# Moving one block's PSUM copies from ScalarE to VectorE, and splitting the last copy and store

## Chip, cores, metric

The kernel runs on one core of a Trainium2 chip. The metric is device time in microseconds (us) of one execution; medians of several executions are given. All executions here are of the undisturbed ("fast") state. The profile is of one execution and its span is about 1.7 us shorter than that execution's device time. Engines: PE is TensorE's matmuls, PEld its weight loads, DVE is VectorE, ACT ScalarE, SPq the queue from which SyncE issues stores.

## The reference

A depthwise causal convolution over seven taps (weights softmaxed per head) is followed by a two-layer feed-forward network with a leaky ReLU:

```python
x_unf = x_pad[:, idx, :].reshape(B, S, K, H, group)      # B=8, S=4096, D=192, H=8, K=7
x = np.einsum('hk,bskhg->bshg', w, x_unf).reshape(B * S, D)
h = x @ w_in                                             # 192 -> 2048
g = np.maximum(0.01 * h, h)
out = (g @ w_out).astype(np.float32)                     # 2048 -> 192
```

## The kernel before

The work is cut into blocks of 512 positions of two batch rows. VectorE convolves (tile `yt`, three chunks of channels, seven steps each), TensorE multiplies by `w_in` into `ph` in PSUM, ScalarE applies the leaky ReLU (`g`), TensorE multiplies by `w_out` into `po`, and a copy brings each finished sum of 128 positions from PSUM to `o_sb`, whence two sums at a time are stored. Blocks 0 to 4 run as two groups of 256, so that TensorE gets its first work early; from block 5 a group is a whole block of 512.

Which engine makes the copy depends on the block:

```python
NHALF = 5
...
def evac_o(n):
    b, e, s = subs[n]                       # block, batch row, 128 positions in the block
    ...
    o_sb = osb[n // 2]
    copy = nc.scalar.copy if b < NHALF else nc.vector.tensor_copy
    copy(out=o_sb[:, n % 2, :], in_=po.pop(n))
    if n % 2 == 1:                          # store two sums together, 192 KB
        nc.sync.dma_start(out=..., in_=osb.pop(n // 2))
```

In the timelines here VectorE and ScalarE run their instructions in the order in which they are written (in the kernel before ScalarE's copy at 121.25 us, below, stands between two pairs of activations). In each step `j` of a group the first matmuls come first, then the second matmuls with the copies that they finish, then the convolution of the next group:

```python
for j in range(steps):
    for u in range(2 * j, 2 * j + 2):
        mm1(grp, u)                         # TensorE -> ph, ScalarE -> g
    for _ in range(quota):
        mm2_slot(slot); slot += 1           # TensorE -> po; evac_o(n) where a sum is done
    ...
    for job in ahead[per * j : per * (j + 1)]:
        job()                               # VectorE: convolution of the next group
```

`ph` has two buffers and `po` four. A copy of one of these sums therefore stands in its engine's queue in front of the convolution steps of the same step `j`.

## Time and profile before

| | before |
|---|---|
| median, 5 executions | 698.27 us (697.35 to 700.79) |
| span of the profile | 696.7 us |
| TensorE busy | 688.9 us, 99% |
| VectorE, ScalarE busy | 542.4 us, 512.3 us |
| TensorE's waits after 100 us | one: 0.83 us on `yt`, ends at 118.99 |
| start of the last copy to the end of the span | 693.07 to 696.7, 3.63 us |

ScalarE's rhythm in block 5, from its timeline (start us, duration us, group, and in brackets the idle time before it and what ended it):

```profile
119.42 1.94 ACT L364 ACTIVATE g<-ph 128x1024 bf16<-128x1024 f32 x2 [1.48 <-PE ph L357]
121.25 0.33 ACT L416 COPY o_sb<-po 128x192 f32<-128x192 f32 x1
121.44 1.97 ACT L364 ACTIVATE g<-ph 128x1024 bf16<-128x1024 f32 x2
123.58 1.94 ACT L364 ACTIVATE g<-ph 128x1024 bf16<-128x1024 f32 x2 [0.16 <-PE ph L357]
```

Four activations and one copy take 123.58 - 119.42 = 4.16 us, two TensorE steps. ScalarE looks full, and yet it waits 0.16 us for TensorE. The last copy, from VectorE's timeline, and the last four stores, from the list of transfers (count, KB each, median us from issue to landing):

```profile
693.07 0.36 DVE L416 COPY o_sb<-po 128x192 f32<-128x192 f32 x1 [0.96 <-PE po L377]
```

```profile
out_dram<-o_sb SPq DMA_DIRECT2D x4, 192.0 KB, 2.0
```

### The profile page before, as it was taken

Reading aid. Unit: us, or ns where it says so; the run is one execution under the profiler, and the core shown is the slowest. Engines: PE = TensorE matmul, PEld = TensorE weight load, DVE = VectorE, ACT = ScalarE, POOL = GpSimd, SP = SyncE. Lnnn points to the kernel's source line nnn. Section 1 sums busy time; section 2 is a strip of 40 time slices with the busy share of each in tenths; the row PEclk is TensorE's granted clock in tenths of the full one; section 3 lists DMA queues with packets and bytes.
Section 4 is the critical chain, followed back from the end, with each engine's and each line's share of the span. In section 5 each row is a group of like instructions: output and inputs, shape, how many; then the busy total and the mean of one; then the engine's idle time right before and its main releaser. Section 6 shows DMA issues by size and latency. Waiting matters only on the chain.

```text
span 696.7 us, 26003 instructions
## 1 busy us (share of the span) xinstructions
PE 688.9 (99%) x11756; PEld 611.7 (88%) x11756; DVE 542.4 (78%) x1000; ACT 512.3 (74%) x576; POOL 142.2 (20%) x199
## 2 busy tenths in 40 slices
PE   8999999999999999999999999999999999999997
PEld 6899998678888888888888888888888888888887
DVE  6899999867777787777787777787777787777712
ACT  6788887977777777777777777777777777777770
POOL 4732221320222220222211222220222210000000
PEclk9999999999999999999999999999999999999999
DMA  9987563754556545556644556544566535122112
GB/s 172 110 106 84 83 88 68 83 77 80 73 67 92 81 70 81 74 67 93 81 67 85 67 74 92 80 73 74 73 75 86 87 66 73 56 52 58 47 36 70
DMA packets 184847, 54.39 MB, mean 78 GB/s; under 512 B 148384, under 2 KB 184736, under 8 KB 184736
## 3 DMA queue, kind: packets, MB, share of 16 engines
q0 software_dynamic: 98768, 14.17, 29.4%
q1 hardware_dynamic: 85968, 38.56, 23.0%
q8 instruction: 92, 1.51, 0.9%
q14 instruction: 19, 0.16, 0.1%
HBM read 29.88 MB, written 25.17 MB: 79 GB/s over the span
## 4 chain that ended last, share of the span: by engine, by line
PE 83%; DVE 12%; DMA 3%; issue 1%; POOL 0%; ACT 0%; POOLq 0%; ACTq 0%
PE po L377 43%; PE ph L357 40%; DVE yt L182 11%; DMA w_out<-in_moe_w_out_dram 2%; DVE yt L176 1%; DMA w_in<-in_moe_w_in_dram 1%; POOL sel L228 0%; ACT g L364 0%; DVE xt L157 0%; POOL sel L226 0%; DVE o_sb L416 0%; POOL ident masks.py:199 0%; PE ptr L143 0%; POOL ident masks.py:197 0%; POOLq masks.py:199 0%
## 5 line engine op out<-in xcount | busy, mean ns | idle before, releaser
L364 ACT ACTIVATE g<-ph 128x1024 bf16<-128x1024 f32 x512 | 496.4, 1021 | 162.9 <-PE ph L357 162.9
L182 DVE SCALAR_TENSOR_TENSOR yt<-xt,wk,yt 128x512 bf16<-128x512 bf16 (+1 forms) x648 | 442.6, 683 | 17.6
L377 PE MATMUL po<-w_out,g 64*128 64x192 bf16 (+1 forms) x8048 | 398.2, 243 | 0.7 <-DMA w_out<-in_moe_w_out_dram 0.7
L377 PEld LDWEIGHTS <-g 64*128 64x128 bf16 (+1 forms) x8048 | 372.5, 94 | 29.4 <-issue 1.1
L357 PE MATMUL ph<-yt,w_in 64*128 64x512 bf16 (+1 forms) x3552 | 392.2, 347 | 2.3 <-ACT g L364 0.9
L357 PEld LDWEIGHTS <-w_in 64*128 64x128 bf16 x3552 | 250.1, 94 | 47.0 <-issue 5.3
L79 POOL DMA_DIRECT2D x_bf<-in_x_dram x180 | 133.6, 777 | 420.0 <-DMA xt<-x_bf 420.0
L416 DVE COPY o_sb<-po 128x192 f32<-128x192 f32 x216 | 77.3, 358 | 127.2 <-PE po L377 124.8
L176 DVE TENSOR_SCALAR yt<-xt,wk 128x512 bf16<-128x512 bf16 (+1 forms) x108 | 36.8, 340 | 0.2
L416 ACT COPY o_sb<-po 128x192 f32<-128x192 f32 x40 | 13.1, 327 | 0.0
L201 PE MATMUL acc<-xt,diag 64*64 64x256 bf16 x84 | 6.6, 319 | 0.0
L201 PEld LDWEIGHTS <-diag 64*64 64x64 bf16 x84 | 5.1, 126 | 1.4 <-issue 0.6
L250 PE MATMUL warm<-zero 128*128 128x256 bf16 x18 | 4.3, 399 | 1.1 <-DVE junk L218 1.1
L238 POOL DMA_DIRECT2D w_in<-in_moe_w_in_dram x8 | 5.1, 644 | 0.0
L157 DVE COPY xt<-ptr 128x384 bf16<-128x384 bf16 x7 | 2.2, 354 | 2.4 <-PE ptr L143 2.4
L250 PEld LDWEIGHTS <-zero 128*128 128x128 bf16 x18 | 2.0, 131 | 2.2 <-DVE junk L218 1.1
L296 ACT ACTIVATE diag<-ident,wkl 128x64 bf16<-128x64 bf16 x14 | 3.6, 336 | 0.0
L128 DVE CAST x_bf<-x_nat 128x384 bf16<-128x384 f32 x5 | 2.4, 499 | 1.4 <-DMA x_nat<-in_x_dram 1.4
L461 POOL COPY pjunk<-g 1x1 bf16<-1x1 bf16 x1 | 0.2, 177 | 12.0 <-ACT g L364 12.0
L128 ACT CAST x_bf<-x_nat 128x384 bf16<-128x384 f32 x3 | 1.5, 506 | 1.5 <-DMA x_nat<-in_x_dram 1.5
L317 ACT ACTIVATE yt<-acc,rsum 128x256 bf16<-128x256 f32 x2 | 0.9, 473 | 2.2 <-PE acc L201 2.2
L255 ACT ACT_TABLE_LOAD x1 | 1.3, 1283 | 0.8 <-PEq L498 0.8
(29 smaller groups left out, 13.7 us busy)
## 6 DMA issues: line engine op xcount, KB each, us to landing
out_dram<-o_sb SPq DMA_DIRECT2D x128, 192.0 KB, 2.1
x_bf<-in_x_dram POOLq DMA_DIRECT2D x180, 64.0 KB, 3.2
x_nat<-in_x_dram SPq DMA_DIRECT2D x8, 192.0 KB, 4.8
w_in<-in_moe_w_in_dram POOLq DMA_DIRECT2D x8, 192.0 KB, 8.7
xt<-x_bf SPq DMA_TRANSPOSE x90, 2.5
w_out<-in_moe_w_out_dram POOLq DMA_DIRECT2D x1, 768.0 KB, 14.7
w<-in_weight_dram SPq DMA_DIRECT2D x1, 0.2 KB
```

What stands on the lines that cost most here:

```text
L79: nc.gpsimd.dma_start(out=t[:, c, :, e, :], in_=src[2 * rp + e, :, :, c * CH : (c + 1) * CH],)
L128: copy(out=x_bf[q // 2][:, :, h * HS : (h + 1) * HS, e, :], in_=x_nat[q][:, e, :, :].rearrange("p s (c k) -> p c s k", c=NCH),)
L176: lambda s=src, d=dst, c=c: nc.vector.tensor_scalar_mul(d, s, wk[:, c, 0:1])
L182: lambda s=src, d=dst, c=c, k=k: nc.vector.scalar_tensor_tensor(out=d, in0=s, scalar=wk[:, c, k : k + 1], in1=d, op0=mybir.AluOpType.mult, ...
L201: lambda k=k, p=p, a=a, e=e, ps=ps: nc.tensor.matmul(out=acc[ps, :T], lhsT=diag[c][ps, p, k, :], rhs=xt[0][ps, c, a : a + T], start=(k == ...
L238: nc.gpsimd.dma_start(out=w_in[e * CH : (e + 1) * CH, :, fs], in_=moe_w_in[:, fs].rearrange("(c p) f -> p c f", p=CH),)
L250: nc.tensor.matmul(out=wa[:, 0, 0:HT], lhsT=zero[:, 0:128], rhs=zero, start=True, stop=True)
L296: act = nc.scalar.activation(out=diag[c][:, 1, k, :], in_=ident2, func=mybir.ActivationFunctionType.Copy, scale=wkl[:, c, k : k + 1],)
L357: nc.tensor.matmul(out=ph[:, e, i * T : (i + 1) * T], lhsT=w_in[ps, c, f * 128 : (f + 1) * 128], rhs=y[ps, c, t0 : t0 + T], start=(c == 0) ...
L364: act = nc.scalar.activation(out=g[blk][:, nf * u : nf * (u + 1), :, t0 : t0 + T], in_=ph.rearrange("p e (i t) -> p i e t", i=nf), func=my ...
L377: ins = nc.tensor.matmul(out=po[m], lhsT=g[b][ps, fc, e, s * 128 : (s + 1) * 128], rhs=w_out[ps, fc, :], start=(rt != 1 and fc == 0), stop ...
L416: copy(out=o_sb[:, n % 2, :], in_=po.pop(n))
```

## The change

Its intent, as far as the edit tells: relieve ScalarE in block 5, where it is nearly full, by giving block 4's eight copies to VectorE, and shorten the end by letting two engines share the last copy and by storing the last two sums one by one.

```diff
-        copy = nc.scalar.copy if b < NHALF else nc.vector.tensor_copy
-        copy(out=o_sb[:, n % 2, :], in_=po.pop(n))
-        if n % 2 == 1:
+        copy = nc.scalar.copy if b < NHALF - 1 else nc.vector.tensor_copy
+        acc = po.pop(n)
+        if n == NSUB - 1:
+
+            nc.vector.tensor_copy(out=o_sb[:, 1, 0 : D // 2], in_=acc[:, 0 : D // 2])
+            nc.scalar.copy(out=o_sb[:, 1, D // 2 : D], in_=acc[:, D // 2 : D])
+        else:
+            copy(out=o_sb[:, n % 2, :], in_=acc)
+        if n >= NSUB - 2:
+            t0 = st * ST + s * 128
+            nc.sync.dma_start(
+                out=out_rows[2 * rp + e, t0 : t0 + 128, :], in_=o_sb[:, n % 2, :]
+            )
+        elif n % 2 == 1:
```

## The prediction

> **What bounds the kernel now.** I read the page first, then the table of stretches, then the waits of TensorE, then the timelines of TensorE and VectorE in the one stretch where the table has a hole, and last the end of the program.
>
> The chain on the page gives TensorE 83% and VectorE 12%:
>
> ```profile
> PE 83%; DVE 12%; DMA 3%; issue 1%; POOL 0%; ACT 0%; POOLq 0%; ACTq 0%
> ```
>
> The table of stretches (length, then busy time of PE, PEld, DVE, ACT, POOL, clock, DMA share, GB/s) says where they change over:
>
> ```profile
> 100.00:110.00 10.00, 10.00 (x219) 10.00 (x216) 9.50 (x18) 8.55 (x12) 3.44 (x5) 1.00 0.76 82
> 110.00:120.00 10.00, 9.17 (x182) 8.35 (x178) 9.56 (x15) 7.08 (x11) 0.49 (x1) 1.00 0.32 80
> 120.00:130.00 10.00, 9.93 (x140) 6.26 (x136) 9.55 (x14) 9.68 (x14) 3.97 (x6) 1.00 0.83 88
> ```
>
> VectorE is at 9.5 of 10 there with no wait; the rest is issue gaps. TensorE has a hole at 110 to 120, and from 120 ScalarE is nearly full. After 140 TensorE is busy without a break until its last matmul. Its list of waits from 100 us on has one entry, 0.8 us on `yt`. TensorE's timeline shows it (start, duration, group, idle before):
>
> ```profile
> 112.27 1.51 PE L357 MATMUL ph<-yt,w_in 64*128 64x256 bf16 x24
> 113.58 1.52 PE L377 MATMUL po<-w_out,g 64*128 64x192 bf16 x32
> 114.90 1.51 PE L357 MATMUL ph<-yt,w_in 64*128 64x256 bf16 x24
> 116.21 1.52 PE L377 MATMUL po<-w_out,g 64*128 64x192 bf16 x32
> 117.53 0.63 PE L357 MATMUL ph<-yt,w_in 64*128 64x512 bf16 x4
> 118.99 1.04 PE L357 MATMUL ph<-yt,w_in 64*128 64x512 bf16 x8 [0.83 <-DVE yt L182]
> ```
>
> At 117.53 block 5 begins, the first block of full 512-wide groups. Its first two pairs use chunks 0 and 1 of the convolution, the third waits for chunk 2. VectorE's timeline shows that chunk's end:
>
> ```profile
> 108.88 0.35 DVE L176 TENSOR_SCALAR yt<-xt,wk 128x512 bf16<-128x512 bf16 x1
> 109.26 4.69 DVE L182 SCALAR_TENSOR_TENSOR yt<-xt,wk,yt 128x512 bf16<-128x512 bf16 x6
> 113.86 0.35 DVE L176 TENSOR_SCALAR yt<-xt,wk 128x512 bf16<-128x512 bf16 x1
> 114.25 4.69 DVE L182 SCALAR_TENSOR_TENSOR yt<-xt,wk,yt 128x512 bf16<-128x512 bf16 x6
> ```
>
> 114.25 + 4.69 = 118.94, and TensorE goes on at 118.99. So until 119 us the end of the program hangs on VectorE, with no slack at all, and afterwards on TensorE. That is exactly where block 4's sums are copied out.
>
> The end: the last sum is copied by VectorE from 693.07 to 693.43, its store (with the sum before it, 192 KB) is issued at 693.46, and the span ends at 696.7. Stores land 2.0 us after issue.
>
> [...] A copy that waits for its sum therefore holds up every convolution step behind it. The trace agrees: at 142.75 VectorE's first copy has 4.64 us of idle time before it, released by TensorE, and the next convolution step starts only at 143.03, 0.28 after the copy's start. [...] ScalarE's half-copy waits for the count that VectorE's half-copy raises. [...]
>
> **Part 1: block 4's eight copies go from ScalarE to VectorE.** By the built order the first (call it sum 32) comes after five of seven steps of chunk 1 of block 5, the next (33) six steps later, three steps before the end of chunk 2. Sum 34 comes directly after block 5's convolution; 35, 36 and 37 after six steps each of block 6, with three steps left; 38 and 39 in block 7. A full step takes 0.787 us start to start, a copy that need not wait 0.28 (142.75 to 143.03).
>
> When is a sum ready? At 142.75 the copy starts 0.93 after its group of sum matmuls began (141.82); its last matmul is the 16th there, as it is for sums 32 to 37. So I add 0.93 to the group's start.
>
> - Sum 32: VectorE gets there when the sixth step of chunk 1 would have started, 109.26 + 4 x 0.787 = 112.41. The sum is ready at 113.58 + 0.93 = 114.51. Wait 2.10, copy 0.28: everything behind it is 2.38 later.
> - Sum 33: reached at 116.61 + 2.38 = 118.99, ready at 116.21 + 0.93 = 117.14. No wait, 0.28. Block 5's chunk 2 ends 2.66 later, at 121.60, and TensorE resumes at 121.65. **First loss: 2.66 us**, all on the path, since slack was nil.
> - Sum 34: its matmul group began at 119.85, now 122.51, ready 123.44. VectorE stands idle from 121.6: 1.84, plus 0.28. Block 6's first step moves from 118.86 to 123.72, by 4.86.
> - Sums 35, 36, 37: reached at 128.0, 132.5, 137.0; ready at 127.7, 131.9, 136.0. No wait, 3 x 0.28 = 0.84.
> - Block 6's convolution ended at 133.9; now 133.9 + 4.86 + 0.84 = 139.6. TensorE began block 6 at 135.19 and needed its chunk 2 two pairs later, 135.62; shifted by 2.66 that is 138.28. It waits again until 139.65. **Second loss: 1.37 us**, so 139.65 - 135.62 = 4.03 in all.
> - Sums 38 and 39 let VectorE wait again (38 by some 1.9 us), but block 7's steps then fall into the rhythm of all later blocks (three steps, 2.36, and a copy, 0.28, per TensorE step of 2.62). By that rhythm block 7's chunk 2 ends at about 159.9, and TensorE needs it at 160.6: no third loss.
>
> What ScalarE gains is hidden. In block 5 a TensorE step takes (135.19 - 120.51) / 7 = 2.10 us, against 0.66 + 1.31 = 1.97 of matmul work; at most 7 x 0.13 = 0.9 us could come back, and ScalarE's copies alternate with waits on `ph`, so they are not the whole cause. But arriving earlier at block 6 only lengthens the second wait, because VectorE sets its end. I count 0.
>
> **Part 2: the last sum in halves.** A half-copy saves 96 columns: about 0.10 us on VectorE (358 to 258 ns), 0.08 on ScalarE (327 to 247). Because they run one after the other with some 0.05 between, copying takes 0.258 + 0.05 + 0.247 = 0.56 instead of 0.36: +0.20. The last store is 96 KB instead of 192. In the last 7 us the stores move at 300 to 325 GB/s, so halving saves about 0.3 of the landing at most[...]. I take -0.25. Together -0.05: a wash.
>
> **Sum:** 697.73 + 4.03 - 0.05 = 701.7 us.
>
> **Rivals.**
> (a) *The intended gain.* ScalarE is 9.68 of 10 busy at 120 to 130, so unloading it could return up to 0.9 us, and the tail 0.3: 696.5. For it: ScalarE's load. Against: VectorE is the engine with nil slack just before, and the copies land in its queue.
> (b) *The copies cost only their own time.* If sums 32 and 34 were ready when VectorE comes, block 5 would start 2 x 0.28 = 0.56 later, block 6 would not wait, and the ScalarE gain could show: 697.4 to 698.3. Against: sum 32's matmuls begin at 113.58, after VectorE is there (112.41). This ordering comes from the trace, so I hold it unlikely.
> (c) [...] TensorE's idle gap grows from 0.83 to about 3.5 us. [...] one chance in ten.
> (d) *The tail alone.* If the halves overlap or the small store lands much faster, -0.5; if the extra handover is slow, +0.3. It moves the sum little either way.
>
> **Range and chances.** The arithmetic of Part 1 is good to a few tenths, run to run scatter likewise (697.35 to 697.73 in two runs, one at 700.79); (c) stretches the upper side. 700.3 to 703.4. A change of 2% is 14 us; nothing here comes near. Faster 0.005, within 2% 0.985, slower 0.01.
>
> **What would show it.** In the changed kernel: VectorE's first copy at about 114.5 with some 2.1 us idle before it, released by TensorE; a TensorE wait on `yt` of about 3.5 us ending near 121.6; a copy at about 123.4 with 1.8 idle before it; a second TensorE wait on `yt` of about 1.4 near 139.6; the last ScalarE copy starting only after VectorE's ends; the last matmuls some 4 us later. Wrong would be: a single wait on `yt` of about 1.4 (then rival b), none or a shorter block 5 (a), or a clock under 1.00 near 122 (c).

## The result

| | before | changed |
|---|---|---|
| median, 5 executions each | 698.27 us | 703.92 us (702.24 to 705.44) |
| span of the profile | 696.7 us | 700.9 us |
| TensorE's waits on `yt` after 100 us | 0.83 | 3.35 and 0.65 |
| mean granted clock in the executions | 0.999 (the profiled one) | 0.998, 0.994, 0.997, 0.995, 0.995 |
| last copy's start to the end | 3.63 | 3.48 |

The ratio is 1.0073, with a 95% interval of 1.0046 to 1.0101: the mean time of one kernel's fast runs over that of the other's of the same rounds, so it is not quite the ratio of the medians. The change makes the kernel about 5 us slower, which is within 2%.

VectorE's timeline in the changed kernel, around block 4's copies (columns as above; lines between are left out):

```profile
108.44 3.11 DVE L182 SCALAR_TENSOR_TENSOR yt<-xt,wk,yt 128x512 bf16<-128x512 bf16 x4
114.17 0.36 DVE L422 COPY o_sb<-po 128x192 f32<-128x192 f32 x1 [2.62 <-PE po L377]
...
118.51 0.35 DVE L422 COPY o_sb<-po 128x192 f32<-128x192 f32 x1
118.78 2.32 DVE L182 SCALAR_TENSOR_TENSOR yt<-xt,wk,yt 128x512 bf16<-128x512 bf16 x3
124.10 0.36 DVE L422 COPY o_sb<-po 128x192 f32<-128x192 f32 x1 [3.00 <-PE po L377]
```

Where six convolution steps followed each other without a break before, VectorE stops after the fifth of chunk 1's seven steps (the four in the first line, after a first one on L176) and waits 2.62 us for sum 32. It waits again, 3.00 us, for sum 34. TensorE's timeline shows what this does to it:

```profile
115.84 1.52 PE L377 MATMUL po<-w_out,g 64*128 64x192 bf16 x32
117.16 0.63 PE L357 MATMUL ph<-yt,w_in 64*128 64x512 bf16 x4
121.15 1.57 PE L357 MATMUL ph<-yt,w_in 64*128 64x512 bf16 x8 [3.35 <-DVE yt L182]
122.48 1.52 PE L377 MATMUL po<-w_out,g 64*128 64x192 bf16 x16
...
138.77 0.61 PE L357 MATMUL ph<-yt,w_in 64*128 64x512 bf16 x4
140.04 1.04 PE L357 MATMUL ph<-yt,w_in 64*128 64x512 bf16 x8 [0.65 <-DVE yt L182]
```

The wait at block 5 has grown from 0.83 to 3.35 us, and there is a second one at block 6. And the matmuls right after the first wait are slow: eight of them last 1.57 us, where the same eight at 140.04 last 1.04. The table of stretches says why (length; busy time of PE, PEld, DVE, ACT, POOL; the last three columns are granted clock, DMA share and GB/s):

```profile
121.00:121.50 0.50, 0.35 (x4) 0.22 (x5) 0.10 (x1) 0.00 (x0) 0.50 (x1) 1.00 0.93 58
121.50:122.00 0.50, 0.50 (x6) 0.19 (x2) 0.00 (x0) 0.42 (x1) 0.50 (x2) 0.52 1.48 94
...
124.50:125.00 0.50, 0.50 (x5) 0.20 (x3) 0.47 (x2) 0.00 (x0) 0.00 (x0) 0.57 0.69 43
125.00:125.50 0.50, 0.50 (x8) 0.30 (x6) 0.50 (x1) 0.29 (x1) 0.00 (x0) 1.00 0.07 4
```

The clock is halved from about 121.5 to 124.9 us. That is why sum 34 comes late and its copy waits 3.00.

ScalarE, relieved of its copies, keeps the same rhythm:

```profile
129.37 3.89 ACT L364 ACTIVATE g<-ph 128x1024 bf16<-128x1024 f32 x4 [0.27 <-PE ph L357]
133.52 3.89 ACT L364 ACTIVATE g<-ph 128x1024 bf16<-128x1024 f32 x4 [0.26 <-PE ph L357]
```

Four activations per 4.15 us, as before with the copy among them; only the wait on `ph` is longer. The end of the program, from the timeline, and its stores from the list of transfers:

```profile
697.42 0.26 DVE L419 COPY o_sb<-po 128x96 f32<-128x96 f32 x1 [0.96 <-PE po L377]
697.72 0.24 ACT L420 COPY o_sb<-po 128x96 f32<-128x96 f32 x1 [12.97 <-DVE o_sb L419]
```

```profile
out_dram<-o_sb SPq DMA_DIRECT2D x2, 96.0 KB, 1.6
```

The halves run one after the other: ScalarE's starts 0.04 us after VectorE's ends.

### The profile page after: what moved, and what is told of

It is laid out like the page before. It is cut to its first block, busy times and chain, and to the rows that moved or that the text cites.

```text
span 700.9 us, 26010 instructions
## 1 busy us (share of the span) xinstructions
PE 689.9 (98%) x11756; PEld 615.2 (88%) x11756; DVE 543.5 (78%) x1008; ACT 511.4 (73%) x569; POOL 142.3 (20%) x199
## 4 chain that ended last, share of the span: by engine, by line
PE 94%; DMA 3%; DVE 2%; ACT 1%; POOL 0%; issue 0%; DVEq 0%; POOLq 0%
PE po L377 48%; PE ph L357 45%; DMA w_out<-in_moe_w_out_dram 2%; DVE yt L182 2%; DMA w_in<-in_moe_w_in_dram 1%; ACT g L364 1%; DVE o_sb L422 0%; POOL sel L228 0%; DVE yt L176 0%; POOL sel L226 0%; POOL ident masks.py:199 0%; DVE o_sb L419 0%; ACT o_sb L420 0%; POOL ident masks.py:197 0%; PE ptr L143 0%
## 5 line engine op out<-in xcount | busy, mean ns | idle before, releaser
L357 PEld LDWEIGHTS <-w_in 64*128 64x128 bf16 x3552 | 253.1, 94 | 48.4 <-issue 8.6
L422 DVE COPY o_sb<-po 128x192 f32<-128x192 f32 x223 | 79.6, 357 | 129.7 <-PE po L377 127.3
L176 DVE TENSOR_SCALAR yt<-xt,wk 128x512 bf16<-128x512 bf16 (+1 forms) x108 | 36.2, 335 | 0.2
L422 ACT COPY o_sb<-po 128x192 f32<-128x192 f32 x32 | 10.5, 327 | 0.0
```

Source lines behind the costliest of these rows:

```text
L176: lambda s=src, d=dst, c=c: nc.vector.tensor_scalar_mul(d, s, wk[:, c, 0:1])
L357: nc.tensor.matmul(out=ph[:, e, i * T : (i + 1) * T], lhsT=w_in[ps, c, f * 128 : (f + 1) * 128], rhs=y[ps, c, t0 : t0 + T], start=(c == 0) ...
L422: copy(out=o_sb[:, n % 2, :], in_=acc)
```

## The experiments

Theory: VectorE reaches the copies of sums 32 and 34 before the sums are ready, its queue stops, and TensorE pays twice on `yt`; the long gap lets the clock fall. Rivals: the copies' own time on VectorE is what costs; the tail costs; the clock falls for another reason.

Times carry a scatter of some 0.5 us and now and then 3 us (the kernel before: 697.25 to 702.10), so I also compare the traces by one number each: the time from the start of block 5's first 512-wide matmul to the start of the last copy. It leaves out the start-up, which varies (that matmul started between 116.9 and 120.1 us), and the tail, which is given apart.

| kernel | median us | before, same rounds | ratio | block 5 to last copy (trace) | tail (trace) | waits on `yt` (trace) | executions with clock under 0.999 |
|---|---|---|---|---|---|---|---|
| before | | | | 575.54 | 3.63 | 0.83 | 5 of 44 |
| changed | 703.92 | 698.27 | 1.0073 | 580.26 | 3.48 | 3.35, 0.65 | 5 of 5 |
| tail only | 698.17 | 698.15 | 0.9992 | 575.35 | 3.48 | 0.64 | 0 of 6 |
| block 4 only | 702.89 | 698.15 | 1.0058 | 579.08 | 3.57 | 3.36, 0.90 | 3 of 6 |
| all but sum 32 | 700.27 | 698.15 | 1.0025 | 577.23 | 3.61 | 1.64, 0.81 | 1 of 6 |
| copies later | 698.64 | 698.15 | 1.0000 | 575.15 | 3.62 | 0.50 | 1 of 6 |
| keep warm | 702.47 | 697.93 | 1.0059 | 578.95 | 3.52 | filled (0.29 left), 0.77 | 0 of 5 |
| changed, again | 703.56 | 697.93 | 1.0078 | 581.09 | 3.52 | 3.35, 0.41 | 5 of 6 |
| store alone | 698.16 | 697.93 | 1.0011 | 575.78 | 3.36 | 1.08 | 2 of 6 |
| alone, early | 698.35 | 697.93 | 1.0003 | 575.41 | 3.35 | 0.38 | 1 of 5 |
| later and alone | 698.38 | 698.69 | 1.0006 | 575.91 | 3.36 | 1.27 | 2 of 6 |
| only sum 32 | 702.13 | 698.69 | 1.0055 | 580.57 | 3.55 | 3.22 | 6 of 6 |
| only sum 34 | 699.44 | 698.69 | 1.0016 | 575.67 | 3.62 | 0.53, 0.35 | 2 of 6 |
| keep warm, again | 701.99 | 697.80 | 1.0058 | 578.94 | 3.49 | filled (0.29 left), 0.77 | 1 of 6 |

All gave correct results. Intervals of the ratios are 0.002 to 0.003 either side. The tails use the span as it is printed, to 0.1 us; with the unrounded spans of the packed traces they are 3.58 to 3.59 us for every old tail, 3.48 to 3.49 for the changed one and 3.31 for the last two sums stored alone with a whole copy. The mean clock falls below 0.999 also through drops in the start-up: the traces of "alone, early" and "only sum 34" have one at 25 to 30 us, after a wait of 2.04 and 2.12 us for `w_out`. The half clock after the last matmul counts in it too (in the kernel before from 695.9 us to the end at 696.7); it alone brings the profiled execution of the kernel before to 0.999.

### Tail only

The change without its first line: `b < NHALF` is kept.

```diff
-        copy = nc.scalar.copy if b < NHALF - 1 else nc.vector.tensor_copy
+        copy = nc.scalar.copy if b < NHALF else nc.vector.tensor_copy
```

> Only the tail of the change: last sum copied in two halves, last two sums stored alone; block 4's copies stay on ScalarE. Theory (the tail is a wash, the loss is all in block 5 and 6): the halves run one after the other and end 0.18 us later than one copy would (0.258 + 0.04 + 0.238 against 0.358), the small store lands in 1.6 instead of 2.0 us; span from the last copy's start to the end 3.48 instead of 3.63, so about 0.15 us faster than before, not to be told from it by time. No new wait on yt, clock as before (0.999). Rival (the tail's new waits cost what was lost): several us slower.

Measured: same time, 3.48 us of tail against 3.63 (0.10 less with the spans unrounded), one wait on `yt` of 0.64. As expected; the tail is not where the time went.

### Block 4 only

```diff
-        copy = nc.scalar.copy if b < NHALF else nc.vector.tensor_copy
+        copy = nc.scalar.copy if b < NHALF - 1 else nc.vector.tensor_copy
```

> Only block 4's eight copies on VectorE, tail as before. Theory: the whole loss, 4 to 6 us slower than before; VectorE's copy of sum 32 with 2.1 to 2.6 us idle before it, a TensorE wait on yt of about 3.4 us, a half-rate clock[...] just after it, sum 34's copy with 2 to 3 us idle before it, a second wait on yt of 0.5 to 1.4. Rival (the tail): same as before.

Measured: 4.7 us slower by the medians. The trace happened to catch an execution with full clock (1.00), in spite of the gap, so it shows the two waits by themselves:

```profile
121.74 1.04 PE L357 MATMUL ph<-yt,w_in 64*128 64x512 bf16 x8 [3.36 <-DVE yt L182]
...
139.45 1.04 PE L357 MATMUL ph<-yt,w_in 64*128 64x512 bf16 x8 [0.90 <-DVE yt L182]
```

Between block 5 and the last copy 579.08 - 575.54 = 3.54 us are lost, and 3.36 + 0.90 - 0.83 = 3.43 of them are these waits. The copies of sums 32 and 34 waited 1.95 and 1.85 us. The expected wait of 2.1 to 2.6 for sum 32 was a little too high. The half-rate clock is not certain: 3 of 6 executions had it.

### All but sum 32

```diff
-        copy = nc.scalar.copy if b < NHALF else nc.vector.tensor_copy
+        copy = nc.scalar.copy if n <= (NHALF - 1) * 2 * SUB else nc.vector.tensor_copy
```

> Sums 33 to 39 on VectorE, sum 32 stays on ScalarE, tail as before. Theory (it is the wait in front of the copy of sum 32, not the copies' own time, that makes the long gap, and the gap that drops the clock): first TensorE wait on yt 0.83 + 0.28 = 1.1 us, no clock drop, sum 34's copy still waits about 1.8 us, second wait on yt about 1.2 us: some 1.5 us slower than before. Rival (the copies' own time, 0.28 each, is what counts): nearly the loss of the full change for seven of eight copies, that is 4 us or more, or the clock drops here as well.

Measured: 2.1 us slower by time, 1.69 by the trace. The first wait was 1.64 and not 1.1, since sum 33 was not ready either, which the expectation had overlooked: VectorE, no longer held up by sum 32, reached that copy at 116.60 and waited 0.89 us for it. The copy of sum 34 waited 1.84, as expected. No clock drop in the trace. Seven of the eight copies cost less than half; the rival of the copies' own time falls.

### Only sum 32

```diff
-        copy = nc.scalar.copy if b < NHALF else nc.vector.tensor_copy
+        copy = nc.scalar.copy if b < NHALF and n != (NHALF - 1) * 2 * SUB else nc.vector.tensor_copy
```

> Only sum 32 is copied by VectorE, the other seven of block 4 by ScalarE; tail as before. Theory (the first loss alone): copy of sum 32 with 2.0 to 2.6 us idle before it; wait on yt at block 5 about 3.1 us, that is 0.28 less than in the changed kernel (sum 33's copy); no second wait on yt; in some executions a half-rate clock after it. In the trace 2.4 us lost if the clock holds, up to 4 if it drops; time 2 to 4 us slower than before. Rival (losses need all the copies): under 1 us.

Measured: 3.4 us slower for one moved copy of 0.36 us. VectorE's and TensorE's timelines:

```profile
113.99 0.36 DVE L416 COPY o_sb<-po 128x192 f32<-128x192 f32 x1 [1.82 <-PE po L377]
```

```profile
116.98 0.63 PE L357 MATMUL ph<-yt,w_in 64*128 64x512 bf16 x4
120.83 1.89 PE L357 MATMUL ph<-yt,w_in 64*128 64x512 bf16 x8 [3.22 <-DVE yt L182]
```

There is no second wait, as expected. All six executions had a low clock. In the trace the clock is halved from 119.9 to 126.7, and 5.0 us are lost between block 5 and the last copy, more than the 4 I allowed: of these, 3.22 - 0.83 = 2.4 are the wait and the other 2.6 lie in the stretch of half clock, which no second wait absorbs here.

### Only sum 34

```diff
-        copy = nc.scalar.copy if b < NHALF else nc.vector.tensor_copy
+        copy = nc.scalar.copy if b < NHALF and n != (NHALF - 1) * 2 * SUB + 2 else nc.vector.tensor_copy
```

> Only sum 34 is copied by VectorE, the other seven by ScalarE; tail as before. Theory (the second loss alone): first wait on yt as before (0.6 to 1.1 us), copy of sum 34 with about 1.84 us idle before it, block 6's convolution 2.1 us later, second wait on yt 0.1 to 0.7 us because block 6 had 1.7 us of slack; clock full; 0.1 to 0.7 us slower than before. Rival (the wait costs in full): 2.1 us.

Measured: a first wait of 0.53, slightly under what I expected, a copy that waited 1.85, a second wait of 0.35, and 0.13 us lost by the trace (0.75 by the medians, where scatter is as large). VectorE lost 2.1 us and TensorE a sixth of that (the second wait of 0.35), because block 6 had slack that block 5 had not. The same stall of VectorE is worth 2.4 us in one place and next to nothing in the next.

### Copies later

All eight copies on VectorE, but written behind the convolution steps of their step:

```diff
-        copy(out=o_sb[:, n % 2, :], in_=po.pop(n))
+        acc = po.pop(n)
+        if b == NHALF - 1:
+            late.append(lambda: finish_o(n, copy, o_sb, acc))    # copy and store
+        else:
+            finish_o(n, copy, o_sb, acc)
 ...
             for job in ahead[per * j : per * (j + 1)]:
                 job()
+            while late:
+                late.pop(0)()
```

(with `b < NHALF - 1` as in the change)

> All eight copies of block 4 on VectorE, but each is put behind the convolution steps of its TensorE step instead of before them, so that its sum is ready when VectorE comes; tail as before. Theory: VectorE's copies have no idle before them in block 5 and 6 (or under 0.3 us), the first wait on yt is 0.83 + 0.28 = 1.1 us, the second is gone, the clock stays full: 0.0 to 0.5 us slower than before. If unloading ScalarE gives TensorE anything in block 5 it must show here: up to 0.9 us faster. I expect nothing of it, since two TensorE steps of block 5 took 4.16 us before and take 4.16 after the change. Rival (the copies' own time on VectorE): as slow as the full change.

Measured: ratio 1.0000. In block 5 and 6 no copy waits:

```profile
116.93 0.35 DVE L427 COPY o_sb<-po 128x192 f32<-128x192 f32 x1
119.43 0.35 DVE L427 COPY o_sb<-po 128x192 f32<-128x192 f32 x1
121.53 0.35 DVE L427 COPY o_sb<-po 128x192 f32<-128x192 f32 x1
```

The same eight copies on the same engine cost nothing once they stand where their sum is ready. So it was the place in the queue, not the work. And unloading ScalarE gives nothing visible: four activations start every 4.16 us here too. By the trace the stretch is 0.4 us shorter than before, but the first wait is 0.33 us shorter as well, because TensorE came later to block 5.

### Keep warm, and the changed kernel again

The changed kernel with matmuls on zeros in the gap; they add exact zeros to sums that are open:

```diff
+                if blk == NHALF and u == 0 and c == 1:
+                    for _ in range(28):
+                        for e in range(2):
+                            ps = slice(e * CH, (e + 1) * CH)
+                            nc.tensor.matmul(
+                                out=ph[:, e, 0:HT], lhsT=zero[ps, 0:128], rhs=zero[ps, :],
+                                start=False, stop=False,
+                            )
```

> The changed kernel with 28 pairs of matmuls on zeros (256 columns, about 3.0 us, adding nothing to the sums) put into TensorE where it waits for chunk 2 of block 5. Theory (the idle gap of 3.4 us halves the clock, and that is what the prediction's sum lacks): the clock stays full after the gap, sum 34's copy waits about 1.8 us instead of 3.0, second wait on yt about 1.4 us, and the kernel is about 3.8 us slower than before, 1 to 2 us faster than the changed kernel. Rival (the clock drops for another reason, or the drop is paid only in the second wait): clock and time as the changed kernel's.

The kernel it is to be compared with, without an edit:

> The changed kernel again, on the same chip as the run with filler matmuls. Theory: 4 to 7 us slower than before[...]: mean clock of the runs between 0.994 and 0.998, the slower run the lower its clock.

Measured, on the same chip: 702.47 with the filler, 703.56 without. That difference of the medians is no larger than the scatter, so clock and trace decide. The clock was at 0.999 or 1.0 in all five executions with the filler, and lower in five of six without. The trace with the filler:

```profile
117.56 3.26 PE L368 MATMUL ph<-zero 64*128 64x256 bf16 x56
121.11 1.04 PE L357 MATMUL ph<-yt,w_in 64*128 64x512 bf16 x8 [0.29 <-DVE yt L182]
```

Eight matmuls take 1.04 us again, sum 34's copy waits 1.85 instead of 3.00, and the loss from block 5 to the last copy is 578.95 - 575.54 = 3.41, as in the lucky trace of "block 4 only". The second wait (0.77) is below the 1.4 expected. In the new trace of the changed kernel the clock is halved for longer, from 119.7 to 126.5, and the loss is 5.55. So the drop costs 580.26 - 578.95 = 1.3 us when it lasts about 3.4 us, and 581.09 - 578.95 = 2.1 when it lasts about 6.8. It is the idle gap that brings it: filling the gap and nothing else removes it (low clock in 1 of 11 executions with the filler, both runs, against 19 of 23 without). That the slower execution always has the lower clock did not hold (704.27 at 0.998).

Why the drop follows some gaps and spares others was not tested by a run of its own. What follows describes the 14 traces and nothing beyond them; the ends of matmuls in them are modelled. The changes of the clock lie on a grid of steps of 3.41 us, whose place against the program differs from trace to trace: each drop that ends within a trace lasts 3.413 or 6.827 us, and full clock between two drops a whole number of such steps (in "changed" the drops begin at 121.52 and 701.78 us, with 576.85 us of full clock between them, 169 steps of 3.413). The views below are of steps of this grid (`prof LABEL --windows A:B,... --engine PE`: length, PE busy, granted clock, DMA share, GB/s), two each of "changed", "changed, again", "block 4 only" and the start-up of "alone, early":

```profile
118.10:121.51 3.41, 0.36 (x4) 1.00 0.62 83
121.51:124.93 3.42, 3.42 (x30) 0.50 1.45 94
...
116.30:119.71 3.41, 1.22 (x24) 1.00 0.24 53
119.71:123.12 3.41, 2.25 (x16) 0.50 1.38 124
...
116.59:120.01 3.42, 1.79 (x38) 1.00 0.38 77
120.01:123.42 3.41, 1.68 (x26) 1.00 1.01 111
...
22.34:25.75 3.41, 1.37 (x20) 1.00 0.90 63
25.75:29.17 3.42, 3.42 (x32) 0.50 1.32 84
```

After a step in which TensorE was idle for 3.05, 2.19 or 2.04 us the clock is halved (0.50). In "block 4 only" the edge of a step cuts the gap into 1.63 and 1.73 us, and the clock stays full, in the second step and after it. Over all steps that began at full clock in the 14 traces, program ends included, each of the 19 with 1.99 us of idle time or more was followed by half clock, and none with 1.73 or less was. A halved step with idle time in it (1.16 us in "changed, again", 0.91 in "only sum 32") was followed by another, one without by full clock. By this reading a gap of 3.35 us is spared only if the edge leaves less than some limit on both sides; with the limit between the 1.73 and 1.99 us of these traces I estimate that for (2 x 1.73 - 3.35) / 3.41 = 3% to (2 x 1.99 - 3.35) / 3.41 = 18% of its places, and 4 of 23 executions were spared.

The timed executions with the filler stood 4.5 us above before, the trace 3.4. The last run asked why.

> The keep-warm kernel again, for a second trace: its timed runs were about 1 us slower than its profiled one, all at full clock. Theory (the two waits are tied to TensorE's own progress, so a later arrival at block 5 passes through to the end, where the kernel before absorbs part of it): from the first 512-wide matmul of block 5 to the last copy again 579.0 (within 0.3) and the waits as in the first trace, whatever the arrival is; the span then moves with the arrival, which was 116.9 to 120.1 us in the traces so far. Rival (something after block 5 varies): that stretch differs by 0.5 us or more at full clock. Clock of all executions 0.999 or more.

Measured: the stretch is 578.94, against 578.95; the waits are the same; TensorE reached block 5 at 117.57 instead of 117.13, and the last copy started 0.43 us later. Whatever the start-up loses passes through. In traces with the old order the wait shrinks when TensorE comes late (0.64 at 118.57, 0.83 at 117.53, 1.08 at 117.16), so part is absorbed. With sum 32 on VectorE it does not (3.35 at 117.16, 3.36 at 117.75, 3.35 at 116.89): VectorE waits for a sum of TensorE's, and TensorE for VectorE, so the gap is fixed. That the timed executions are slow by late arrivals is consistent with this, but they have no trace, so it stays an inference. One execution had a clock of 0.997, which I had not expected; without a trace of it I can't say where.

### Store alone; alone, early; later and alone

Three tries for a kernel that is better than both. The first stores the last two sums singly, with a whole last copy:

```diff
-        if n % 2 == 1:
+        if n >= NSUB - 2:
+            t0 = st * ST + s * 128
+            nc.sync.dma_start(
+                out=out_rows[2 * rp + e, t0 : t0 + 128, :], in_=o_sb[:, n % 2, :]
+            )
+        elif n % 2 == 1:
```

> Kernel before, but the last two sums stored each alone; the last copy in one piece on VectorE. Theory (of the tail only the smaller store is a gain): last copy's start to the span's end about 3.25 to 3.3 us instead of 3.63, so 0.35 us faster than before and 0.2 faster than the tail of the change. Rival: the landing of the last store does not depend on its size; 3.63.

Measured: a tail of 3.36 instead of 3.63 (0.27 less with the spans unrounded); in the time it is lost in scatter. The second takes two early copies off VectorE as well:

```diff
-                evac_first(3, nc.vector.tensor_copy, nc.vector.tensor_copy)
+                evac_first(3, nc.scalar.copy, nc.scalar.copy)
```

> As the store-alone kernel, and two copies of transposed input (the fourth half block, about 0.35 us each) moved from VectorE to ScalarE in the first 30 us. Theory (VectorE carries the path until 119 us with no slack): the wait on yt at block 5 shrinks from 0.83 to about 0.1 us, and the kernel is about 1.0 us faster than before. Rival (ScalarE's queue holds the copies up, and VectorE or TensorE waits for them): same or slower, with a new wait before 30 us.

A miss: ratio 1.0003. The wait on `yt` did shrink to 0.38, but TensorE came late to block 5 (120.04), and at 120.11 "only sum 34" had a wait of 0.53 without this edit, so little of that is shown to be its work. In the traced execution VectorE had also waited for its input:

```profile
45.92 0.28 DVE L176 TENSOR_SCALAR yt<-xt,wk 128x256 bf16<-128x256 bf16 x1 [3.66 <-DMA xt<-x_bf]
```

Neither ScalarE's queue nor VectorE's load was the next limit there, but the transposed input. That execution was also the slowest of its kernel, with a late start-up, so I don't claim that this wait is in all of them. The third joins "copies later" and "store alone":

> The later-copies kernel with the last two sums stored alone, the last copy whole on VectorE. It joins what did no harm: from the first 512-wide matmul of block 5 to the start of the last copy about 575.2 us (before: 575.5, changed kernel: 580.3), from there to the end 3.36 (before 3.63). Theory: as fast as before within scatter, about 5 us faster than the changed kernel, and by the trace some 0.3 to 0.6 us better than before, which the times can't tell. Rival (copies on VectorE cost as such): 1 us or more slower than before.

Measured: 698.38 against 698.69, a tail of 3.36, and 575.91 between block 5 and the last copy. The stretch is longer than the 575.2 I expected, since TensorE arrived early and waited 1.27. It is 5 us better than the changed kernel and the same as before. No version here beats the kernel before by more than the scatter.

## Why the prediction was right or wrong

It was right in direction, place and the mechanism of the two waits, and wrong about the clock: it said a loss of 4.0 us, and the medians say 703.92 - 698.27 = 5.65. The median lies 0.5 us above the range's upper end of 703.4; the ratio applied to the 697.73 that the prediction started from gives 702.8, inside it. That is in part luck: the range reached so far up only for rival (c), to which the prediction gave one chance in ten. By its steps:

- **First loss, 2.66 us.** TensorE's wait came out at 3.36 and 3.35, against 0.83 + 2.66 = 3.49 foretold. Removing sum 32 alone from VectorE took away the long gap, and sum 32 alone brought it. Shown.
- **Second loss, 1.37 us.** The mechanism was right, the size too large: 0.90 in the trace with full clock ("block 4 only"). VectorE needed 17.7 us from the end of block 5's convolution to that of block 6's, not 18.0, and TensorE was 0.2 slower than I shifted it. Together the two losses measured 3.5 us instead of 4.03.
- **ScalarE's gain, counted as 0.** Right, and for a stronger reason than the one given: I held that the gain would be hidden by the second wait. In "copies later", where nothing hides it, the rhythm stays at 4.16 us per two steps. The pace there follows the round trip between TensorE and ScalarE through the two `ph` buffers, by my reading (ScalarE waits 0.16 us for TensorE on `ph` in the kernel before and 0.26 to 0.27 in the changed one); that round trip was not tested by itself.
- **The tail, -0.05 us.** Measured -0.10 in the traces of the changed tail. The copies ran in series as the built order said (0.26 + 0.04 + 0.24), and the small store landed 0.4 us earlier (96 KB in 1.6 us, 192 KB in 2.0), more than the 0.25 taken. The 258 and 247 ns of the half copies and the 0.05 us between them were my estimates; the traced halves took 258 and 238 ns with 0.04 us between, the whole copies 358 on VectorE and 327 on ScalarE.
- **Rival (b), the copies' own time.** Fallen: ratio 1.0000 with all eight on VectorE behind their steps.
- **Rival (c), a halved clock after the gap, at "one chance in ten".** This is the step that failed. The one chance in ten, like the 703.4 us that went with it, was my estimate and not shown by a run. The five executions of the changed kernel had low clocks, and so did five of six more; of all 23 executions with the long gap unfilled (changed, changed again, block 4 only, only sum 32) it was 19, against 5 of 44 for the kernel before. In the traces 2.19 us of idle time in a step of 3.41 was enough, so a gap of 3.35 us seldom passes: the one chance in ten was near that of being spared. The drop should have been the expected case, worth 1.3 to 2.1 us, and the sum about 703.

What stays open: where between 1.73 and 1.99 us of idle time in a step such a limit lies, whether it explains the executions without a trace, and the last microsecond between the timed executions of "keep warm" and its trace.

## What to carry to other kernels

An instruction moved to an engine with spare capacity takes a place in that engine's queue, and everything behind it waits for its input: here one copy of 0.36 us waited 2.62 us for its sum, and the convolution behind it stood still. Before moving one, work out from the trace when the engine would get there and when the input is ready, and put it behind work that does not need it. A wait that two engines hold against each other was paid in full here (3.35, 3.36 and 3.35 us on `yt`, whenever TensorE arrived). If a change makes TensorE idle, look at the granted clock after the gap: with the unfilled gap (3.22 to 3.36 us in the traces) 19 of 23 executions had a mean clock under 0.999, and in the traces 1.99 us of idle time in one step of the clock's grid were enough.
